# Weight low parts on VectorE alone, constant products that read ones, and a new order of work

## The chip, the core and the metric

The kernel runs on one core of a Trainium2 chip. A core has TensorE (PE in the profile; its weight loads are listed as PEld), VectorE (DVE), ScalarE (ACT), GpSimd (POOL) and SyncE (SP), which issues the transfers. Each engine works through its own instructions in program order and waits by semaphores for the others. The metric is the device time of one execution in microseconds, as a median over several runs.

## The reference

Two stages, one behind the other. The first is clustered attention on `q`, `k`, `v` of shape 4 x 8 x 768 x 64 (batch, heads, tokens, head size) with 16 centroids a head:

```
q_assign = argmax(normalised q . normalised centroids)      # the same for k
mask     = q_assign[:, None] == k_assign[None, :]
scores   = where(mask, (q @ k.T) / sqrt(64), -1e9)
attn     = exp(scores - max);  attn = attn / (sum(attn) + 1e-9)
out      = attn @ v
```

The second takes the 3072 tokens of 512 values that come of it, as `x`, through two large products with a rational function between them:

```
h = x @ w_in                                                # 3072 x 2048
g = (a0 + a1 h + a2 h^2 + a3 h^3) / (1 + |b0||h| + |b1| h^2 + 1e-6)
out = g @ w_out                                             # 3072 x 512
```

`w_in` (512 x 2048) and `w_out` (2048 x 512) come as 64-bit floats. They and all large operands are split into a high and a low part of 16 bits, and a product is the sum of three: high by high, high by low, low by high.

## The kernel before

**The order is written out by hand.** Nothing runs while the kernel is described: each step is a call of `op`, which appends it to a plan (`Plan`, 4453 steps). `emit` then walks through `ORDER`, a list of 4453 numbers, and issues the steps in that sequence. The rows of an engine's instructions stand in the order in which its steps come in that list. A step may issue several instructions.

**The weights** (`weights`, called eight times: four column groups of `w_in`, named `wi0` to `wi3`, four row groups of `w_out`, `wo0` to `wo3`; four tiles of 128 x 512 in each, 32 in all). A tile is loaded as 64-bit words into `rwi...` or `rwo...` (512 KB; L423; two buffers), and is made a 32-bit float in `wwi...` or `wwo...`: ScalarE takes the magnitude of the upper words (`m...`), VectorE shifts it and joins it with bits of the lower words (L558, L565), ScalarE takes the sign (`g...`), GpSimd multiplies the two (L574). TensorE then forms the squares of a group's four tiles, and of their sum `root_pow2` makes a scale, a power of two (`wis`, `wos`; its last steps are L496 and L499 on VectorE). With the scale ScalarE writes the high part, `win[:, 0]` or `wout[:, 0]`, and the **low part**, scaled value minus high part, is formed in one of two ways:

- tiles 1 and 3 of a group: one VectorE instruction, L626, that scales and subtracts;
- tiles 0 and 2: two GpSimd instructions, L635, which scales in place, and L642, which subtracts.

Which it is, `share("wdl", c)` decides: with `K['wdl']` at 0.5 it is true for tiles 1 and 3. So of the 32 low parts 16 are VectorE's and 16 GpSimd's. All are written while the first batch's attention runs, and the second stage needs them.

**The first batch** (`prep`, `attend_keys`). Each of its four head pairs is scaled: ScalarE sums squares of `k` and `q` over a row (`sumk`, `sumq`), TensorE turns the sum into a row (`kt`, L1013), VectorE takes its largest value (`km`, L1015), TensorE spreads that to all partitions (`kb`, L1017), and VectorE makes scales of it (`ksc`, `qsc`, L1027 to L1070). The scaled `tk` and `tq` are transposed (for the first pair on TensorE, L980, with `ident16`). Then come the scores, their largest values, a second run of scores, and the values `px` (L1323 in the later batches, L1501 and L1507 in the first). Of `px` the results are made through `rw`: VectorE L1529 and L1536, TensorE, then VectorE L1553, one set for each head pair and each third of the tokens (`rw_1_0`: pair 1, first third). They end as `x` (GpSimd, L1561). The later batches (`attend`) use scores `s` (L1243), their smallest value (VectorE L1272), the exponential (ScalarE) and `ah`, the split result (ScalarE, then VectorE L1303), which frees the scores' bank.

**The second stage** (`moe`) runs for thirds of a batch: `ph` = x @ w_in (L1612), the rational function (ScalarE, VectorE L1630, L1637, L1731, GpSimd L1677, L1750), `po` = g @ w_out (L1761). It reads columns `gk` of numbers that `g_scale` makes from the scales of the weights, of `v` and from `moe_a`, `moe_b`, in small GpSimd steps (L850, L899, L902). The second stage of one batch runs among the attention of the next.

**The constant products** (`warm`, 16 calls). Each call is a group of eight TensorE products 128 x 128 whose result nobody reads (L786). They read `ident16`, an identity in 16 bits, which VectorE casts from `ident` (L390). TensorE's first instructions are eleven such groups.

Of the kernel before, what the change touches and what calls it, by code (L numbers as in the profile page):

```python
# [57 lines left out]
K = {'xn': 14, 'scp': 1, 'vsc': 0.75, 'sup0': 0, 'stk': 2, 'lop': 0, 'mgp': 0, 'rvn': 2, 'at': 3, 'vn': 3, 'ah': 5, 'sua': 1.0, 'T1': 1, 'quick': 1, 'sqd': 0.0, 'gld': 0.0, 'gp': 0.3, 'pp': 0.0, 'NR': 19, 'acb': 1.0, 'warm': 16, 'fast': 16, 'pet': (0,), 'wdl': 0.5}  # L58
# [200 lines left out]
def clustered_attention_moe_kernel(  # L259
# [75 lines left out]

    def kshare(name, b, i):
        return share(name if f"{name}.{b}" not in K else f"{name}.{b}", i)

    TOGETHER = kn('together', ())

    KEYMAJOR = {(b, hp) for b in range(B) for hp in range(kn("km", (4, 0, 0, 0))[b])}

    plan.look = kn("look", 40.0)
    NM = 2
    NR = kn("NR", 12 if kn("gw", 1) == 1 else 6)

    def misc(shape, dt, name):
# [1506 lines left out]
```

## Time and profile before

| | |
|---|---|
| median of 3 runs | 903.31 us (903.31 to 904.04) |
| the profiled execution, its own time | 900.24 us |
| span of its instructions | 898.4 us |
| busy: TensorE, VectorE, ScalarE, GpSimd | 862.0, 811.3, 794.5, 533.2 us |
| granted TensorE clock over the span | 0.99 |

The profile is of one execution, which took 900.24 us; the span leaves out 1.8 us around its first and last instruction. "Busy" counts an engine's instructions, not its waits, and says nothing of how well an engine is used: TensorE's matmuls overlap and their ends are modelled. A table by stretches of the span gives the same busy time for parts of it. A table of waits gives the idle time of an engine ahead of an instruction and what ended it. A timeline lists instructions in order of their start.

### The profile page before, as it was taken

To read this page: it belongs to the slowest core of one execution; us is meant where nothing else is said; L and a number is where in the kernel's file an instruction comes from. 1 tells how busy PE (TensorE), PEld (TensorE's weight loads), DVE (VectorE), ACT (ScalarE), POOL (GpSimd) and SP (SyncE) were. 2 spreads that over 40 slices of the span, in tenths; PEclk is the share of its full clock that TensorE was granted. 3 is DMA by queue.
4 is the path that set the end of the run, shared out by engine and by line. 5 is a ranking of instruction groups with operands and counts; after the bars stand their busy time and mean duration, and the time that the engine had idled before them with its cause. 6 is when DMAs were issued, how large, how long until landed. Compare 5 with 4: busy or idle time off the path is not lost.

```text
span 898.4 us, 20920 instructions
## 1 busy us (share of the span) xinstructions
PE 862.0 (96%) x7893; PEld 594.4 (66%) x7893; DVE 811.3 (90%) x1610; ACT 794.5 (88%) x1497; POOL 533.2 (59%) x530
## 2 busy tenths in 40 slices
PE   5699999988999999999999999999999999999998
PEld 4566777765666666657667666667676666767654
DVE  3999989789999999989999999999999998877793
ACT  4688899999999999999999999999999999895652
POOL 2337645677766385547556737565666555687664
PEclk9799999999999999999999999999999999999999
DMA  4698876779877999886979999989789875150000
GB/s 155 190 251 216 198 186 144 206 146 210 160 139 139 191 198 183 190 161 127 216 153 167 178 189 171 159 169 179 152 154 170 156 139 95 36 95 1 24 24 24
DMA packets 353013, 135.76 MB, mean 151 GB/s; under 512 B 327824, under 2 KB 344208, under 8 KB 352912
## 3 DMA queue, kind: packets, MB, share of 16 engines
q1 hardware_dynamic: 352912, 134.42, 74.0%
q8 instruction: 62, 1.02, 0.4%
q14 instruction: 39, 0.32, 0.1%
HBM read 41.98 MB, written 6.29 MB: 54 GB/s over the span
## 4 chain that ended last, share of the span: by engine, by line
PE 61%; DVE 17%; ACT 14%; issue 5%; POOL 1%; DMA 1%; SPq 1%; ACTq 0%; DVEq 0%
PE po L1761 20%; PE ph L1612 19%; PE s L1243 7%; PE px L1323 5%; DVE s L1272 3%; ACT s L409 3%; DVE ah L1303 3%; ACT u L409 2%; ACT ah L409 2%; PE s L1386 2%; PE z L1480 2%; PE px L1501 2%; DVE t L1637 1%; DVE t L1630 1%; PE ptl L1138 1%
## 5 line engine op out<-in xcount | busy, mean ns | idle before, releaser
L1612 PE MATMUL ph<-x,win 128*128 128x256 f16 x2304 | 266.2, 273 | 1.1 <-DVE t L1637 0.6
L1761 PE MATMUL po<-wout,g 128*128 128x512 f16 x1152 | 267.1, 379 | 0.0
L1612 PEld LDWEIGHTS <-win 128*128 128x128 f16 x2304 | 223.9, 98 | 42.0 <-DVE t L1637 2.9
L1761 PEld LDWEIGHTS <-g 128*128 128x128 f16 x1152 | 110.5, 98 | 120.1 <-issue 3.4
L1750 POOL TENSOR_TENSOR g<-t,u 128x512 f16<-128x512 f32 x84 | 112.7, 1344 | 93.8 <-DVE t L1743 56.6
L1677 POOL TENSOR_TENSOR s<-s,u 128x512 f32<-128x512 f32 x84 | 111.2, 1329 | 74.9 <-ACT s L409 73.1
L1272 DVE TENSOR_SCALAR_CACHE_REDUCE s<-s,cc 128x768 f32<-128x768 f32 x144 | 144.9, 1018 | 4.4 <-PE s L1243 3.5
L1303 DVE SCALAR_TENSOR_TENSOR ah<-s,su,ah 128x768 f16<-128x768 f32 x144 | 144.1, 1010 | 4.4 <-ACT ah L409 3.9
L409 ACT ACTIVATE ah<-s,su 128x768 f16<-128x768 f32 x144 | 127.8, 899 | 6.6 <-DVE su L1291 6.1
L409 ACT ACTIVATE s<-s,nm 128x768 f32<-128x768 f32 x144 | 125.6, 872 | 8.4 <-DVE s L1272 6.5
L1243 PE MATMUL s<-sk,sq 128*128 128x384 f16 x576 | 115.6, 327 | 6.3 <-DVE ah L1303 5.6
L1243 PEld LDWEIGHTS <-sq 128*128 128x128 f16 x576 | 52.0, 98 | 49.9 <-DVE ah L1303 16.4
L1323 PE MATMUL px<-at,vhi 128*64 128x256 f16 x864 | 73.9, 275 | 1.9 <-DVE s L1731 1.8
L409 ACT ACTIVATE t<-ph,gk 128x512 f32<-128x512 f32 x84 | 65.3, 778 | 0.0
L1630 DVE SCALAR_TENSOR_TENSOR t<-ph,gk,t 128x512 f32<-128x512 f32 x84 | 62.2, 742 | 2.5 <-ACT t L409 1.4
L1637 DVE SCALAR_TENSOR_TENSOR t<-t,gk,ph 128x512 f32<-128x512 f32 x84 | 62.3, 741 | 1.2
L409 ACT ACTIVATE u<-s,cq 128x512 f32<-128x512 f32 x84 | 59.8, 721 | 3.0 <-POOL s L1677 2.9
L409 ACT ACTIVATE s<-u,g 128x512 f32<-128x512 f32 x84 | 60.3, 723 | 0.5
L409 ACT ACTIVATE u<-ph,gk 128x512 f32<-128x512 f32 x84 | 57.7, 688 | 3.3 <-PE ph L1612 3.1
L1731 DVE SCALAR_TENSOR_TENSOR s<-s,g 128x512 f32<-128x512 f32 x84 | 59.8, 714 | 0.5
L1323 PE MATMUL px<-at,vlo 128*64 128x256 f16 x432 | 59.7, 273 | 0.0
L1323 PEld LDWEIGHTS <-vhi 128*64 128x64 f16 x864 | 45.0, 110 | 15.3 <-issue 10.3
(241 smaller groups left out, 1552.4 us busy)
## 6 DMA issues: line engine op xcount, KB each, us to landing
rwi<-in_moe_w_in_dram SPq DMA_DIRECT2D x16, 512.0 KB, 3.9
rwo<-in_moe_w_out_dram SPq DMA_DIRECT2D x16, 512.0 KB, 4.3
rk<-in_k_dram SPq DMA_DIRECT2D x32, 192.0 KB, 3.9
rq<-in_q_dram SPq DMA_DIRECT2D x32, 192.0 KB, 3.7
rvm<-in_v_dram SPq DMA_DIRECT2D x16, 384.0 KB, 4.0
rv<-in_v_dram SPq DMA_DIRECT2D x16, 384.0 KB, 4.1
out_dram<-ob SPq DMA_DIRECT2D x24, 256.0 KB, 2.9
sq<-sq SPq DMA_DIRECT2D x12, 192.0 KB, 4.1
```

The lines of the kernel that those rows point to most:

```text
L409: lambda: nc.scalar.activation(out=out(), in_=in_(), func=func, **{a: (x() if callable(x) else x) for a, x in kw.items()}),
L1243: nc.tensor.matmul(sc.ap[:, i, :SH], lhsT=st["q" + x].ap[:, j, t, :], rhs=st["k" + x].ap[:, j, ks, :].rearrange("p t c -> p (t c)"), start ...
L1272: lambda nm=nm, view=view: ts(out=view(), in0=view(), scalar1=cc.ap[:, 0:1], scalar2=None, op0=ALU.mult, op1=ALU.min, accum_out=nm.ap),
L1303: lambda part=part, view=view, su=su: stt(out=part(1), in0=view(), scalar=su.ap, in1=part(0), op0=ALU.mult, op1=ALU.subtract),
L1323: nc.tensor.matmul(px.ap[j * D : (j + 1) * D, :], lhsT=vv.ap[:, j, kt, :], rhs=at[j].ap[:, p_, kt].rearrange("p t c -> p (t c)"), start=(i ...
L1612: nc.tensor.matmul(ph.ap[:, fi * TW : (fi + 1) * TW], lhsT=win[:, wpart, c, f * P : (f + 1) * P], rhs=xs[c].ap[:, xpart], start=(i == 0), ...
L1630: lambda t=t, h=h, ph=ph, col=col: stt(out=t[h].ap, in0=ph.ap, scalar=col("rho")(), in1=t[h].ap, op0=ALU.mult, op1=ALU.mult),
L1637: lambda t=t, h=h, ph=ph, col=col: stt(out=t[h].ap, in0=t[h].ap, scalar=col("a1")(), in1=ph.ap, op0=ALU.add, op1=ALU.mult),
L1677: lambda uv=uv, sv=sv: nc.gpsimd.tensor_tensor(out=sv(), in0=sv(), in1=uv(), op=ALU.mult),
L1731: lambda sv=sv, g16=g16: stt(out=sv(), in0=sv(), scalar=1.0 + 1e-6, in1=g16(0), op0=ALU.add, op1=ALU.mult),
L1750: lambda tv=tv, uv=uv, g16=g16, e=(nc.vector if kshare("gld", b, i_) else nc.gpsimd): e.tensor_tensor(out=g16(1), in0=tv(), in1=uv(), op=A ...
L1761: nc.tensor.matmul(po[ti].ap, lhsT=g16(gg)[:, c0 : c0 + P], rhs=wout[:, wpart, f, :], start=(i == 0 and f == 0), stop=(i == 2 and f == NF ...
```

## The change

- `K['wdl']` goes from 0.5 to 1.0: L626 (L628 in the new numbering, which is two higher from there) forms all 32 low parts. L635 and L642 are no longer issued: 32 fewer GpSimd instructions, 16 more of VectorE, and 4437 steps for 4453.
- The constant products read `w16w`, a tile of ones in bfloat16 that a VectorE memset fills, for `ident16`. `ident16` is now made on GpSimd (a memset and a select, by `make_identity`), not cast on VectorE.
- `ORDER` is another list from end to end.
- The set `KEYMAJOR` is written in another way and holds the same four head pairs.

```diff
-K = {..., 'warm': 16, 'fast': 16, 'pet': (0,), 'wdl': 0.5}
+K = {..., 'warm': 16, 'fast': 16, 'pet': (0,), 'wdl': 1.0}
...
 ORDER = [int(i) for i in """
+4438 4450 40 41 42 43 4437 4447 4445 4449 4444 4443 4452 4448 44 3 4 74 75 5 6 76 77 78 79 386 387 389 4451
...
-    KEYMAJOR = {(b, hp) for b in range(B) for hp in range(kn("km", (4, 0, 0, 0))[b])}
+    KEYMAJOR = {(0, hp) for hp in kn("kmset", (0, 1, 2, 3))}
...
     ident16 = cp.tile([P, P], F16, name="ident16")
-    nc.vector.tensor_copy(out=ident16, in_=ident)
+    make_identity(nc, ident16)
+    w16w = cp.tile([P, P], BF16, name="w16w")
+    nc.vector.memset(w16w, 1.0)
...
             for _ in range(8):
-                nc.tensor.matmul(wm.ap[:, :P], lhsT=ident16, rhs=ident16, start=True, stop=True)
+                nc.tensor.matmul(wm.ap[:, :P], lhsT=w16w, rhs=w16w, start=True, stop=True)
```

What the new order and the new instructions make of the rows is shown at three places. In a row the name stands ahead of its inputs (`out<-in`); a number at a name's end is that of a buffer and differs between the two kernels for that reason alone.

**The head of VectorE's instructions**, from the second weight tile to the first scale `ksc`. Before:

```order
L444 TENSOR_TENSOR csq<-craw 128x64
L445 TENSOR_REDUCE css<-csq 128x1
L448 TENSOR_SCALAR cn<-css 128x1
L558 TENSOR_SCALAR wwo_1_222<-mwo_1_218 128x512
L565 SCALAR_TENSOR_TENSOR wwo_1_222<-rwo_1_216,wwo_1_222 128x512
L390 CAST ident_85<-ident 128x128
L1015 TENSOR_REDUCE km_0_245<-kt_0_243 1x1
L1027 TENSOR_SCALAR ksc_0_249<-kb_0_247 128x1
```

After (in the new numbering; `w16w` is filled five rows above the first of these):

```order
L560 TENSOR_SCALAR wwi_2_122<-mwi_2_120 128x512
L567 SCALAR_TENSOR_TENSOR wwi_2_122<-rwi_2_118,wwi_2_122 128x512
L560 TENSOR_SCALAR wwo_1_186<-mwo_1_184 128x512
L567 SCALAR_TENSOR_TENSOR wwo_1_186<-rwo_1_182,wwo_1_186 128x512
L446 TENSOR_TENSOR csq<-craw 128x64
L1017 TENSOR_REDUCE km_0_249<-kt_0_247 1x1
L447 TENSOR_REDUCE css<-csq 128x1
L450 TENSOR_SCALAR cn<-css 128x1
L1029 TENSOR_SCALAR ksc_0_264<-kb_0_262 128x1
```

The cast of `ident16` (`ident_85`) is gone from here; `km` stands behind the same two weight tiles as before, and of the centroids' three steps two now come behind it.

**VectorE around the results of the second head pair** (`rw_1_0`, `rw_1_1`), the same row numbers in both. Before:

```order
L1553 SCALAR_TENSOR_TENSOR rw_1_0_1712<-px_1_0_1675,ev_1171,rw_1_0_1712 128x256
L1027 TENSOR_SCALAR qsc_0_1830<-sumq_0_1828 128x1
L1529 SCALAR_TENSOR_TENSOR rw_1_1_1869<-px_1_1_1832,eps,rw_1_1_1869 128x128
L1536 SCALAR_TENSOR_TENSOR rw_1_1_1869<-rw_1_1_1869 128x128
L1015 TENSOR_REDUCE km_0_1890<-kt_0_1888 1x1
L1027 TENSOR_SCALAR ksc_0_1911<-kb_0_1909 128x1
L558 TENSOR_SCALAR wwo_3_1917<-mwo_3_1915 128x512
L565 SCALAR_TENSOR_TENSOR wwo_3_1917<-rwo_3_1913,wwo_3_1917 128x512
L626 SCALAR_TENSOR_TENSOR wout<-wwo_1_1196,wos,wout 128x512
L1040 TENSOR_SCALAR ksc_0_1911<-ksc_0_1911 128x1
L1045 RECIPROCAL ksc_0_1911<-ksc_0_1911 128x1
L1050 TENSOR_SCALAR qsc_0_1830<-ksc_0_1911 128x1
```

After:

```order
L1538 SCALAR_TENSOR_TENSOR rw_1_0_1681<-rw_1_0_1681 128x128
L628 SCALAR_TENSOR_TENSOR win<-wwi_2_1037,wis,win 128x512
L498 TENSOR_SCALAR woe<-wop_ln 128x1
L501 RECIPROCAL wos<-woe 128x1
L1531 SCALAR_TENSOR_TENSOR rw_1_1_1849<-px_1_1_1812,eps,rw_1_1_1849 128x128
L1538 SCALAR_TENSOR_TENSOR rw_1_1_1849<-rw_1_1_1849 128x128
L628 SCALAR_TENSOR_TENSOR wout<-wwo_2_572,wos,wout 128x512
L560 TENSOR_SCALAR wwo_3_1857<-mwo_3_1810 128x512
L1555 SCALAR_TENSOR_TENSOR rw_1_0_1681<-px_1_0_1644,ev_1204,rw_1_0_1681 128x256
L628 SCALAR_TENSOR_TENSOR win<-wwi_3_498,wis,win 128x512
L567 SCALAR_TENSOR_TENSOR wwo_3_1857<-rwo_3_1808,wwo_3_1857 128x512
L560 TENSOR_SCALAR wwo_0_1900<-mwo_0_1898 128x512
```

Where one low part (L626) stood in twelve rows, three stand now (L628), two of `w_in` and one of `w_out`, between the steps of `rw_1_0` and `rw_1_1`.

**GpSimd's steps of `gk`**, the last ones ahead of the first `ph`. Before:

```order
L850 TENSOR_SCALAR gk_2428<-woe,g_2430 128x4
L850 TENSOR_SCALAR g_2430<-g_2430 128x1
L635 TENSOR_SCALAR wwi_2_1487<-wwi_2_1487,wis 128x512
L850 TENSOR_SCALAR g_2430<-g_2430,aab 128x1
L850 TENSOR_SCALAR gk_2428<-gk_2428,g_2430 128x4
L899 TENSOR_TENSOR gk_2428<-gk_2428 128x4
L1561 TENSOR_TENSOR x_2_1_2464<-rw_2_1_2360,x_2_1_2464 128x256
L850 TENSOR_SCALAR gk_2428<-gk_2428,ab 128x4
L642 TENSOR_TENSOR wout<-wwo_2_2049,wout 128x512
L642 TENSOR_TENSOR win<-wwi_2_1487,win 128x512
L850 TENSOR_SCALAR gk_2428<-gk_2428,ab 128x4 x2
L635 TENSOR_SCALAR wwo_2_1344<-wwo_2_1344,wos 128x512
```

After:

```order
L852 TENSOR_SCALAR g_2424<-g_2424 128x1
L852 TENSOR_SCALAR g_2424<-g_2424,aab 128x1
L852 TENSOR_SCALAR gk_2422<-gk_2422,g_2424 128x4
L1563 TENSOR_TENSOR x_1_2_2799<-rw_1_2_1965,x_1_2_2799 128x256
L901 TENSOR_TENSOR gk_2422<-gk_2422 128x4
L852 TENSOR_SCALAR gk_2422<-gk_2422,ab 128x4 x4
L904 TENSOR_TENSOR gk_2422<-gk_2422 128x4
L1563 TENSOR_TENSOR x_3_0_2970<-rw_3_0_2719,x_3_0_2970 128x256
```

The four instructions of low parts (L635, L642) that stood between the `gk` steps are gone, and the result `x_1_2` (L1563) stands there now.

## Rows read from the trace of the kernel before

**Rows 1.** The page, part 1: busy us, share of the span, instructions.

```profile
PE 862.0 (96%) x7893; PEld 594.4 (66%) x7893; DVE 811.3 (90%) x1610; ACT 794.5 (88%) x1497; POOL 533.2 (59%) x530
```

**Rows 2.** Stretches: length, each engine's busy us, then TensorE's clock, DMA share, GB/s.

```profile
0.00:20.00 20.00, 8.80 (x111) 8.12 (x112) 6.08 (x30) 8.39 (x16) 5.05 (x18) 0.99 0.44 140
20.00:60.00 40.00, 32.15 (x324) 23.97 (x326) 37.45 (x99) 29.08 (x52) 12.91 (x13) 0.79 0.82 229
60.00:100.00 40.00, 39.39 (x456) 27.25 (x453) 39.42 (x84) 34.35 (x62) 26.66 (x26) 1.00 0.87 205
100.00:200.00 100.00, 96.30 (x1253) 72.14 (x1252) 86.19 (x196) 94.35 (x183) 59.58 (x74) 1.00 0.75 176
200.00:400.00 200.00, 192.06 (x1648) 129.54 (x1647) 193.59 (x380) 194.23 (x381) 125.52 (x120) 1.00 0.92 177
400.00:880.00 480.00, 479.30 (x4043) 326.90 (x4042) 444.23 (x820) 429.50 (x802) 295.81 (x274) 1.00 0.69 129
```

**Rows 3.** TensorE's waits, 200 to 400 us: sum, times, longest.

```profile
PE s L1243 <- DVE ah L1303: 4.9, 5, 1.9
```

**Rows 4.** Timeline, first 20.5 us: start, length, engine [idle before, releaser].

```profile
0.83 0.17 DVE L374 MEMSET ones<- 128x128 f32 x1 [0.83 <-PEq L1838]
...
8.32 0.69 DVE L565 SCALAR_TENSOR_TENSOR wwo<-rwo,wwo 128x512 int32<-128x512 int32 x1
...
8.93 0.22 DVE L390 CAST ident<-ident 128x128 f16<-128x128 f32 x1
...
9.02 0.19 ACT L409 ACTIVATION_READ_ACCUMULATOR tk<-rk 128x1 f32 x1
...
9.08 0.34 SPq L423 DMA_DIRECT2D rwi<-in_moe_w_in_dram  x1
...
9.21 1.03 PE L786 MATMUL warm-39.99_113<-ident 128*128 128x128 f16 x8 [9.21 <-DVE ident L390]
...
12.60 0.63 PE L786 MATMUL warm-39.92_156<-ident 128*128 128x128 f16 x8
...
15.75 0.27 PE L1013 MATMUL kt<-ident,sumk 128*1 128x128 f32 x1
...
16.05 0.28 DVE L1015 TENSOR_REDUCE km<-kt 1x1 f32<-1x128 f32 x1 [6.90 <-PE kt L1013]
...
19.88 0.66 ACT L409 ACTIVATE mwi<-rwi 128x512 f32<-128x512 f32 x1
```

**Rows 5.** Loads into `rwi`, first 60 us: from issue to landing.

```profile
DMA to landing us min/median/max: 3.6/3.9/5.6
```

**Rows 6.** Lines L626 and L565: ns min/median/max, first and last start.

```profile
L626 DVE SCALAR_TENSOR_TENSOR win<-wwi,wis,win x8: 731/742/1173, 84.1 to 182.4; 128x512 f16<-128x512 f32 x8
L626 DVE SCALAR_TENSOR_TENSOR wout<-wwo,wos,wout x8: 721/744/917, 104.3 to 192.6; 128x512 f16<-128x512 f32 x8
...
L565 DVE SCALAR_TENSOR_TENSOR wwo<-rwo,wwo x16: 674/691/1639, 8.3 to 167.2; 128x512 int32<-128x512 int32 x16
```

**Rows 7.** GpSimd's groups by line and form: busy us, mean ns, idle before.

```profile
L642 POOL TENSOR_TENSOR win<-wwi,win 128x512 f16<-128x512 f32 x8 | 10.9, 1356 | 0.3
...
L642 POOL TENSOR_TENSOR wout<-wwo,wout 128x512 f16<-128x512 f32 x8 | 9.5, 1196 | 0.3
...
L635 POOL TENSOR_SCALAR wwo<-wwo,wos 128x512 f32<-128x512 f32 x8 | 5.8, 722 | 4.1 <-DVE rest L1437 3.2 <-ACT wout L409 0.9
...
L635 POOL TENSOR_SCALAR wwi<-wwi,wis 128x512 f32<-128x512 f32 x8 | 5.7, 711 | 0.1
```

**Rows 8.** Timeline, 181 to 192 us, of GpSimd and of TensorE.

```profile
182.55 0.68 POOL L850 TENSOR_SCALAR gk<-woe,g 128x4 f32<-128x4 f32 x1 [5.66 <-DVE g L894]
...
190.38 1.36 PE L1612 MATMUL ph<-x,win 128*128 128x256 f16 x11
```

**Rows 9.** VectorE's waits, 60 to 200 us.

```profile
DVE rw L1529 <- ACT rw L409: 2.2, 3, 1.1
```

**Rows 10.** A stretch of 5 us, columns as in rows 2.

```profile
30.00:35.00 5.00, 3.38 (x33) 3.41 (x34) 4.89 (x12) 5.00 (x9) 2.49 (x3) 0.50 0.29 89
```

More of the change, by code (lines that the diff above doesn't have):

```diff
@@ L55, in emit @@
             self.ops[i]()
-K = {'xn': 14, 'scp': 1, 'vsc': 0.75, 'sup0': 0, 'stk': 2, 'lop': 0, 'mgp': 0, 'rvn': 2, 'at': 3, 'vn': 3, 'ah': 5, 'sua': 1.0, 'T1': 1, 'quick': 1, 'sqd': 0.0, 'gld': 0.0, 'gp': 0.3, 'pp': 0.0, 'NR': 19, 'acb': 1.0, 'warm': 16, 'fast': 16, 'pet': (0,), 'wdl': 0.5}
+K = {'xn': 14, 'scp': 1, 'vsc': 0.75, 'sup0': 0, 'stk': 2, 'lop': 0, 'mgp': 0, 'rvn': 2, 'at': 3, 'vn': 3, 'ah': 5, 'sua': 1.0, 'T1': 1, 'quick': 1, 'sqd': 0.0, 'gld': 0.0, 'gp': 0.3, 'pp': 0.0, 'NR': 19, 'acb': 1.0, 'warm': 16, 'fast': 16, 'pet': (0,), 'wdl': 1.0}
 ORDER = [int(i) for i in """
[193 rows of a table removed]
[193 rows of a table added]
 """.split()]
```

386 rows, old and new, of the table ORDER are left out of this document.

## The prediction

> **What bounds the kernel now.** Read the busy table first, then the same by stretches of the span, then the waits. TensorE is busy 862.0 us of 898.4, VectorE 811.3 [rows 1]. The stretches tell what that average hides [rows 2]. From 400 to 880 us TensorE is idle 0.7 us of 480: whatever is won or lost before 400 us arrives at the end one for one, and nothing can be won behind it but the last few us. From 200 to 400 us TensorE lacks 7.9 us and VectorE only 6.4; the score products wait there for VectorE's `ah` instruction, which frees their bank (4.9 us in 5 waits [rows 3]). So this stretch goes at VectorE's pace. From 20 to 100 us VectorE is all but full too (2.6 us idle of 40, then 0.6 of 40). From 100 to 200 us it has 13.8 us idle, while TensorE (96.3) and ScalarE (94.4) are nearly full. And at the front, TensorE does 8.8 us of work in the first 20.
>
> The front is one chain. TensorE starts at 9.21 us, because its first constant product reads `ident16`, which VectorE casts at 8.93, behind weight arithmetic that waits for a load [rows 4]. Eleven groups of eight constant products then stand ahead of the first useful transpose, `kt`, and they run to 15.75. ScalarE had the sum that `kt` reads at 9.21 (9.02 + 0.19). VectorE stands still for 6.90 us until 16.05, its next instruction being the one that reads `kt`, and ScalarE waits behind that (all [rows 4]).
>
> **The change, part by part.**
>
> *Constant products read ones.* The new `w16w` is a VectorE memset ahead of everything that waits for a load; the memset of `ones`, same elements, takes 0.17 us and stands at 0.83 [rows 4]. TensorE can start near 1.4. The first four of the eleven groups start 0.85 us apart (9.21 to 12.60 is 3.39), the other seven 0.45 (12.60 to 15.75 is 3.15) [rows 4]: 6.5 us, done at 7.9 instead of 15.75. Last then is ScalarE's sum at 9.21, and `kt` can run at 9.25: 6.5 us earlier. If all eleven ran at the pace of the first four, they would end at 1.4 + 9.35 = 10.75 and the gain be 5.0. I take 6.5, since the pace should rise after as long a run as it did before. One group is moved between `kt` and `kb`; `kb` needs VectorE's `km` first (16.05 + 0.28 [rows 4]), so 0.45 us of it is hidden, 0.85 nearly. The identity moves to GpSimd, as a memset and a select ahead of its first weight tile; nobody waits for it before the transposes of `tk`, which in this trace come after 16.05. What is late next: the load of the third weight tile is issued at 9.08 [rows 4] and lands after a median 3.9 us, at most 5.6 [rows 5]: 13.0 to 14.7. ScalarE reads it at 19.88 [rows 4], so at 13.4 if all moves by 6.5. Median: in time; worst: 1.3 us late. So the front gives 6.5, between 3.7 and 6.5. VectorE being full from 20 to 100 us, work that starts earlier there ends earlier.
>
> *All low parts on VectorE.* Sixteen more instructions of the form of L626, median 742 and 744 ns [rows 6]. Back to back, VectorE's instructions start about 0.08 us before the one ahead has ended (8.32 + 0.69 is 9.01, the next starts at 8.93 [rows 4]), so one costs 0.66 and sixteen 10.6 us; without that overlap 11.9. GpSimd loses 16 pairs, 10.9 + 9.5 + 5.8 + 5.7 = 31.9 us [rows 7], which is worth little in itself: GpSimd is busy 59% [rows 1].
>
> *Where they stand.* By the new order 30 of the 32 low parts are ahead of the first hidden product `ph`, where all 16 of VectorE's were: 14 more, 9.3 us, nearly all of it between the second head pair's results and `ph` at 190 [rows 8]. That is the stretch with 13.8 us of idle VectorE. All of it could be covered, or none. I take 8 of 10.6 us: the stretches where VectorE sets the pace keep 1.4% (60 to 100) to 3.2% (200 to 400) idle [rows 2]; with ScalarE and TensorE nearly full I allow this one some 5%, and 13.8 less 5.8 is 8. So 2.6 us stay on the path. If the cover were gone the whole 10.6 would be, since VectorE sets the pace from 200 to 400.
>
> *Less beside GpSimd.* A VectorE instruction is now and then far longer than its like: L565 has a median of 691 ns and a maximum of 1639, L626 742 and 1173 [rows 6], so one such case costs 0.4 to 0.9 us. If they come from GpSimd's work beside them, they get fewer: from 60 to 200 us GpSimd is busy 86.2 us [rows 2], of which 31.9 go, 37%. I take one case of the longer kind, 1.0 us (0 to three of them, 2.8).
>
> *The chain to `ph`.* GpSimd's small `gk` instructions begin at 182.55 and `ph`, which reads `gk`, at 190.38 [rows 8]; four of the removed instructions stand between them: two of each kind, by the group means 2 x (0.71 + 1.28) = 4.0 us [rows 7]. So `ph` could come up to 4.0 us earlier; but TensorE has other products to do ahead of it and few gaps [rows 2], so I count 0 and keep 4.0 for the low end.
>
> **The sum.** 900.24 us (the profiled execution; span 898.4) - 6.5 + 10.6 - 8.0 - 1.0 = 895.3. The median of the runs, 903.31, lies 3.1 above the profiled one, so 898.4 us.
>
> **Rivals.**
>
> *A. VectorE pays in full; slower.* The 13.8 us idle are waits, in program order, for short steps that go through other engines (the longest in sum is `rw` for ScalarE, 2.2 us in 3 waits [rows 9]). More instructions in that queue delay such a step by as much as they fill, and the gap comes back behind it. For it: the waits are many and short; against it: the new order was laid out with the new instructions in it. 900.24 - 6.5 + 10.6 = 904.3, by the median 907.4. It decides when less than 4.1 us of the 10.6 are covered.
>
> *B. The front's gain stops at the next wait.* If the loads or the work of the second head pair hold the front, 2 us of the 6.5 arrive: 895.3 + 4.5 = 899.8, by the median 902.9, within 0.2%.
>
> *C. More than counted.* All 10.6 covered and half of the 4.0 us and a little more off the chain to `ph`, 2.6: 895.3 - 5.2 = 890.1, by the median 893.2.
>
> *D. The clock.* The granted clock is 0.99 in the first 20 us [rows 2] and 0.50, the lower of its two levels (1.2 of 2.4 GHz), from 30 to 35 [rows 10], after stretches in which TensorE had pauses. Constant products that end at 7.9 leave a pause before `kt` and thin work behind it. TensorE's 32.15 us at 0.79 (20 to 60 us [rows 2]) are 25.4 at full rate; at half rate all the way they need 50.8, 10.8 more than the 40 us they have: 909.2. Against it: VectorE, not TensorE, is full there, and the rate was half for part of it already. The Trainium skill (TensorE: Matmul & The Clock Gate, What's actually happening) says that the throttled state is the default and activity releases it; by that an early run that ends early gains nothing for what comes after. This trace agrees that the rate falls again when the run is over [rows 10].
>
> *E. Held by GpSimd.* The new instruction reads two tiles from SBUF, as L626 does now. Were each held as the worst of L626 (1173 ns, 0.43 over the median [rows 6]): 16 x 0.43 = 6.9, so 905.3. The medians, near the fastest (721 and 731 ns [rows 6]), speak against it. The Trainium skill (SBUF — State Buffer, Who interferes with whom) states that such an instruction and a GpSimd one that reads SBUF exclude each other, and the second waits for the whole of the first. The trace agrees in so far as single cases are long, and in no more: by the medians most were held by nothing.
>
> **How the numbers follow.** My forecast 898.4 has a chance of 0.46, with a range of its own from 895 to 901.4; C 0.16; B 0.14; A 0.16; D 0.04; E 0.04. 0.2% is about what a measurement of this kernel can tell from no change, 901.5 to 905.1. Faster: forecast and C, 0.62. Same: B, 0.14. Slower: A, D, E, 0.24. The range reaches into C and just over A, 892 to 907.5: some 0.06 lie below and 0.12 above.
>
> **What would show it.** First constant product near 1.4 us, `kt` near 9.3, VectorE's wait for it under 1 us. VectorE's idle time from 95 to 190 us at 5 to 6 instead of 13.8; L628 at 32 with a median near 743 ns. The first `ph` some 4 to 6 us earlier than 190.4, and TensorE without gaps from 400 on. I am wrong at the front if `kt` comes early but the first scores don't; at the cover if VectorE's idle time stays above 10 us and `ph` comes near 190; in the rest of the order if `ph` is early and the end is not.

## The result

The changed kernel takes 888.85 us (median; 887.65 to 889.21), the kernel before 903.54 beside it: a ratio of 0.9834 with a 95% interval from 0.9817 to 0.9851, or 15 us. Measured once more in a later series (e13) it is 0.9861 (0.9837 to 0.9885), 12.6 us. The forecast was faster by 4.9 us, at 898.4, with a range down to 892.0: the direction was right, but the time lies below the range, and the forecast gain is a third of what came. The profiled execution took 888.94 us with a span of 886.8; before it was 900.24 and 898.4.

The page of the changed kernel, part 1 (busy us, share of the span, instructions), answers to [rows 1], and the table by stretches to [rows 2] (length, busy us of TensorE, its weight loads, VectorE, ScalarE and GpSimd, then clock, DMA share, GB/s).

```profile
PE 860.9 (97%) x7893; PEld 596.3 (67%) x7893; DVE 818.5 (92%) x1626; ACT 795.1 (90%) x1497; POOL 498.4 (56%) x500
```

```profile
0.00:20.00 20.00, 14.79 (x189) 13.70 (x190) 12.77 (x50) 14.48 (x26) 5.83 (x20) 0.91 0.76 240
20.00:60.00 40.00, 34.82 (x349) 24.83 (x346) 38.06 (x95) 31.05 (x56) 16.00 (x15) 0.87 0.84 215
60.00:100.00 40.00, 39.98 (x508) 28.67 (x509) 39.29 (x88) 33.47 (x61) 15.05 (x16) 1.00 0.82 210
100.00:200.00 100.00, 95.71 (x1199) 72.91 (x1197) 94.50 (x209) 96.07 (x188) 45.08 (x61) 1.00 0.68 174
200.00:400.00 200.00, 193.92 (x1709) 132.57 (x1704) 196.08 (x390) 196.47 (x387) 121.46 (x118) 1.00 0.91 173
400.00:880.00 480.00, 479.32 (x3954) 322.75 (x3952) 437.84 (x799) 422.31 (x784) 295.02 (x272) 1.00 0.68 128
```

From 100 to 200 us VectorE is idle 5.5 us where it was 13.8, and TensorE is as busy as it was. From 400 on nothing is left to win, as before.

The front, from the timeline of its first 20.5 us (start, length, engine, in brackets the idle time before and what ended it), answers to [rows 4]:

```profile
1.18 0.17 DVE L392 MEMSET w16w<- 128x128 bf16 x1
...
1.40 1.03 PE L788 MATMUL warm-39.87_124<-w16w 128*128 128x128 bf16 x8 [1.40 <-DVE mrow L394]
...
9.09 0.27 PE L1015 MATMUL kt<-ident,sumk 128*1 128x128 f32 x1
...
9.40 0.28 DVE L1017 TENSOR_REDUCE km<-kt 1x1 f32<-1x128 f32 x1 [0.60 <-PE kt L1015]
...
14.03 0.66 ACT L411 ACTIVATE mwi<-rwi 128x512 f32<-128x512 f32 x1 [0.22 <-DMA rwi<-in_moe_w_in_dram]
```

Constant products from 1.40 us, `kt` at 9.09 (15.75 before), VectorE's wait for it 0.60 (6.90 before), the third weight tile read at 14.03 after a wait of 0.22 for its load.

The new line of the low parts answers to [rows 6] (ns of one: shortest, median, longest; first and last start), and the first hidden products show how early `ph` is:

```profile
L628 DVE SCALAR_TENSOR_TENSOR win<-wwi,wis,win x16: 733/744/1805, 70.0 to 180.3; 128x512 f16<-128x512 f32 x16
L628 DVE SCALAR_TENSOR_TENSOR wout<-wwo,wos,wout x16: 731/746/1770, 98.0 to 189.4; 128x512 f16<-128x512 f32 x16
...
L1614 PE MATMUL ph<-x,win x120: 269/272/283, 180.5 to 198.6; 128*128 128x256 f16 x120
```

The first `ph` stands at 180.5 us, 9.9 earlier than at 190.38 [rows 8]; from there to the end it is 706.3 us now and was 708.0. So most of the gain is made ahead of `ph`.

### The profile page after: what moved, and what is told of

The parts are those of the page before. It is cut to its first block, busy times and chain, and to the rows that moved or that the text cites. A ratio compares the mean times of both kernels' runs of the same rounds, so it can differ in the third digit from the quotient of the medians.

```text
span 886.8 us, 20919 instructions
## 1 busy us (share of the span) xinstructions
PE 860.9 (97%) x7893; PEld 596.3 (67%) x7893; DVE 818.5 (92%) x1626; ACT 795.1 (90%) x1497; POOL 498.4 (56%) x500
## 4 chain that ended last, share of the span: by engine, by line
PE 64%; DVE 16%; ACT 13%; issue 4%; DMA 1%; POOL 0%; ACTq 0%; DVEq 0%; SPq 0%; POOLq 0%
PE po L1763 21%; PE ph L1614 19%; PE s L1245 7%; PE px L1325 6%; ACT s L411 4%; DVE s L1274 3%; DVE ah L1305 2%; ACT ah L411 2%; PE px L1503 2%; ACT u L411 2%; PE s L1388 2%; PE z L1482 2%; DVE top L1398 1%; PE px L1509 1%; DVE s L1733 1%
## 5 line engine op out<-in xcount | busy, mean ns | idle before, releaser
L1325 PEld LDWEIGHTS <-vhi 128*64 128x64 f16 x864 | 44.7, 110 | 13.9 <-issue 9.2
```

Source lines behind the costliest of these rows:

```text
L1325: nc.tensor.matmul(px.ap[j * D : (j + 1) * D, :], lhsT=vv.ap[:, j, kt, :], rhs=at[j].ap[:, p_, kt].rearrange("p t c -> p (t c)"), start=(i ...
```

## The experiments

The theories that the expectations name: **1**, the front gives 6.5 us and the order covers the 16 instructions; **2**, the relief of GpSimd is a gain of its own; **3**, the early start shortens the time at the lower clock; **4**, the order behind `ph` gains too; **5**, the 16 still cost something in the new order; **6** and **7**, the clock or VectorE's lateness is what misplaced instructions cost.

Four marks are read from every trace: the start of `kt`, of the first values `px`, of the first `ph`, and the span.

| | kt | first px | first ph | span | median | ratio to before (95%) |
|---|---|---|---|---|---|---|
| before | 15.75 | 57.9 | 190.4 | 898.4 | 903.5 | 1 |
| changed | 9.09 | 48.7 | 180.5 | 886.8 | 888.9 | 0.9834 (0.9817 to 0.9851) |
| e1 old order, ones, GpSimd pairs | 9.38 | 52.6 | 184.8 | 892.9 | 895.4 | 0.9921 (0.9902 to 0.9941) |
| e2 old order, identity, VectorE's low parts | 16.25 | 58.4 | 196.1 | 909.3 | 913.1 | 1.0120 (1.0097 to 1.0144) |
| e3 old order, ones, VectorE's | 9.27 | 52.5 | 191.3 | 906.5 | 906.3 | 1.0048 (1.0030 to 1.0066) |
| e4 new order, identity, VectorE's | 16.83 | 56.5 | 187.9 | 894.2 | 896.8 | 0.9942 (0.9924 to 0.9961) |
| e5 new order, ones, GpSimd pairs | 8.22 | 48.1 | 189.7 | 895.7 | 897.8 | 0.9941 (0.9929 to 0.9954) |
| e6 new order to ph, then old | 8.02 | 48.3 | 180.5 | 892.0 | 894.0 | 0.9903 (0.9888 to 0.9919) |
| e7 old order to ph, then new | 9.53 | 51.1 | 190.0 | 904.3 | 906.1 | 1.0028 (1.0012 to 1.0043) |
| e8 changed, the 16 twice | 8.48 | 48.2 | 190.9 | 897.4 | 899.2 | 0.9958 (0.9943 to 0.9972) |
| e9 old order, ones, no low parts of tiles 0, 2 | 9.56 | 52.5 | 183.7 | 891.7 | 893.0 | 0.9896 (0.9880 to 0.9913) |
| e10 new order, ones, none of those | 8.27 | 48.0 | 179.8 | 888.5 | 889.3 | 0.9853 (0.9834 to 0.9871) |
| e11 as e3, the low parts in new places | 9.25 | 52.5 | 194.0 | 905.3 | 907.0 | 1.0050 (1.0034 to 1.0066) |
| e12 changed, the low parts in old places | 8.98 | 48.6 | 184.3 | 896.7 | 898.3 | 0.9950 (0.9931 to 0.9970) |
| e13 changed, again | 8.45 | 48.1 | 179.5 | 886.9 | 890.6 | 0.9861 (0.9837 to 0.9885) |
| e14 as e12, with products in the pauses | 8.73 | 48.5 | 183.7 | 894.6 | 897.2 | 0.9939 (0.9918 to 0.9960) |
| e15 changed, with products in the front's pauses | 8.92 | 48.9 | 179.8 | 886.2 | 890.2 | 0.9856 (0.9832 to 0.9881) |
| e16 changed, 9 groups ahead of kt | 8.58 | 48.1 | 179.7 | 887.2 | 890.3 | 0.9864 (0.9838 to 0.9890) |

The runs were made in four series, each with the kernel before beside it: its median was 901.8 us beside e1 to e4, 903.4 beside e5 to e8, 902.7 beside e9 to e12 and 903.1 beside e13 to e16. So versions of different series are compared by their ratios, and a ratio's interval is some 0.2% wide to either side, 2 us. The marks and spans are those of one profiled execution each.

### The edits one by one

**e1, the ones alone.**

```diff
 (ORDER and K as before)
-    nc.vector.tensor_copy(out=ident16, in_=ident)
+    make_identity(nc, ident16)
+    w16w = cp.tile([P, P], BF16, name="w16w")
+    nc.vector.memset(w16w, 1.0)
...
-    nc.tensor.matmul(wm.ap[:, :P], lhsT=ident16, rhs=ident16, start=True, stop=True)
+    nc.tensor.matmul(wm.ap[:, :P], lhsT=w16w, rhs=w16w, start=True, stop=True)
```

Expected:

> The kernel before, its own order and its own split of the low parts; only the constant products read ones, and the identity is made on GpSimd. Theory 1 (the front is worth 6.5 us and no more; what the change gave beyond it came from the new order): 903.5 - 6.5 = 897.0, with the useful work of TensorE 6 to 6.5 us ahead of before from 25 us on and no more later. Rival, theory 3 (the earlier front also brings the full clock back earlier, which gave the 2 us between 30 and 47 us): 903.5 - 8.5 = 895.0, and the granted clock of 40 to 60 us is 1.00 where before has 0.91. If a load holds the front: 901.

Measured 6.4 us less by the medians of this series (901.8 to 895.4). `kt` comes 6.4 earlier, the first `px` 5.3, `ph` 5.6, the end 5.5. Theory 1 holds: what the front gives arrives at the end but for about 1 us, which is lost ahead of `px`. Theory 3's sign is missing: the granted clock from 40 to 60 us is 0.95 and not 1.00, and over the first 60 us it is 0.86 as before.

**e2 and e3, the low parts on VectorE in the old order,** without and with the ones.

```diff
-K = {..., 'wdl': 0.5}
+K = {..., 'wdl': 1.0}
 ORDER (old), for each of the 16 low parts of tiles 0 and 2:
-    the two GpSimd steps (L635, L642)
+    the one VectorE step, in the place of the second
```

> The kernel before, its own order; only the 16 low parts of tiles 0 and 2 are formed by VectorE, each in the place where the second of its two GpSimd instructions stood. Theory 1 (VectorE pays for what its idle time of 100 to 200 us doesn't cover; only a new order covers it well): 2.6 to 10.6 us more, 906 to 914, VectorE's idle time from 95 to 190 us falling from 12.5 to 6 or less. Rival, theory 2 (the 32 instructions that GpSimd loses gain more than VectorE's 16 cost, in any order): no slower than before, 903.5 or less.

> Both edits of the first two runs together in the old order: the change without its new order. By theory 1 their sum, 900 to 907, so that the new order is worth 11 to 18 us against the changed kernel's 888.9. By theory 2 it is 897 or less and the order is worth 8 or less.

e2 is 11.3 us slower than before, e3 10.9 slower than e1: the 10.6 us of the instructions, paid in full. Theory 2 falls for the old order. Only half of it is paid ahead of `ph`: in e2 `ph` comes 5.7 us later than before and the end 10.9.

**e4, the new order without the ones.**

```diff
 (the changed kernel)
-    make_identity(nc, ident16)
-    w16w = cp.tile([P, P], BF16, name="w16w")
-    nc.vector.memset(w16w, 1.0)
+    nc.vector.tensor_copy(out=ident16, in_=ident)
...
-    nc.tensor.matmul(wm.ap[:, :P], lhsT=w16w, rhs=w16w, start=True, stop=True)
+    nc.tensor.matmul(wm.ap[:, :P], lhsT=ident16, rhs=ident16, start=True, stop=True)
```

> The changed kernel with its new order and its low parts, but the constant products read the identity that VectorE casts, as before. Theory 1 (the front is worth 6.5): 888.9 + 6.5 = 895.4. Theory 3 (the early start also shortens the stretch at the lower clock): 888.9 + 8.5 = 897.4. The difference to the kernel before is then what the new order and the low parts gave together, 6 to 8 us.

The two expected times were worked out from a time of another series. By the ratios e4 is 7 to 10 us behind the changed kernel (0.9942 against 0.9861 and 0.9834), by the spans 7.4, which does not tell 6.5 from 8.5. The granted clock over the first 60 us is 0.89 in both traces, so nothing speaks for theory 3. `kt` comes at 16.83 here, 7.7 later than in the changed kernel. The products start at 9.19, as before, but six of the eleven groups start 0.85 us apart here and only four did before. Yet the first `px` is at 56.5, earlier than before (57.9), though `kt` is 1.1 later. The new order makes up 2.5 us between the two marks.

### What the low parts cost in each order

**e5, GpSimd's pairs in the new order; e8, the 16 twice.**

```diff
 (e5: the changed kernel)
-K = {..., 'wdl': 1.0}
+K = {..., 'wdl': 0.5}
 ORDER (new): the two GpSimd steps where VectorE's one stood
...
 (e8: the changed kernel, L628)
-    lambda hl=hl, wf=wf: stt(...),
+    lambda hl=hl, wf=wf, c=c: [stt(...) for _ in range(2 - c % 2)],
```

> The changed kernel with its new order and its products of ones, but the low parts of tiles 0 and 2 are two GpSimd instructions again, both standing where VectorE's one stood. Theory 1 (the new order covers VectorE's 16 instructions and gains by itself; which engine forms the low parts then matters little): 887 to 890, at most 2 us from the changed kernel. Rival, theory 2 (GpSimd's 31.9 us in these places hold somebody up, so that giving them to VectorE is a gain of its own): 893 to 898. Rival, theory 5 (VectorE's 16 instructions still cost part of their 10.6 us in the new order): 880 to 886.

> The changed kernel with each of the 16 moved low parts formed twice over, one instruction behind the other: 10.6 us more of VectorE in the places where the new order put them. If the new order had cover to spare, 889 to 892; if it is filled by the 16 it has (VectorE's idle time from 85 to 180 us is 5.4 us now), 894 to 900, that is 5 to 10.6 us more.

e5 misses theory 1 and lies in theory 2's range: in the new order GpSimd's pairs do hold somebody up. They cost 8.9 us by the span against VectorE's 16 (8.0 by the ratios against e10 below, which has neither), all of it between `px` (48.1) and `ph` (189.7). Among ScalarE's waits from 95 to 200 us of e5 (what waits, for whom: us in sum, times, longest) are 6 us for GpSimd's second instruction. `gwo`, `rw` and the weight tile that this one reads take their buffers from one ring of 19, and ScalarE waits until one is free:

```profile
ACT gwo L404 <- POOL wout L637: 3.9, 2, 2.0
ACT rw L404 <- POOL win L637: 2.1, 1, 2.1
```

In the changed kernel's waits of that stretch no line of a low part stands. In e8 the 16 instructions a second time cost 9 to 11 us (0.9958 against 0.9861 and 0.9834), their full price, also all ahead of `ph` (190.9). The new order has no room for 16 more.

**e9 and e10, without the low parts of tiles 0 and 2.**

```diff
 (e9: old order; e10: new order; both with the ones)
+    if c % 2 == 0:
+        op("POOL", 500, lambda hl=hl: nc.gpsimd.memset(hl.ap[:, 1], 0.0), [], [hl], vt)
+        continue
```

> Old order, products of ones, and no low parts of tiles 0 and 2 at all (left out of the computation: a GpSimd memset that waits for nothing fills each with zeros). Beside the first run (with the GpSimd pairs, 895.4) and the third (with VectorE's instructions, 906.3) it prices both ways in the old order. If the pairs cost nothing there: 895. If they held something up too: 888 to 893. Either way VectorE's 16 cost the rest up to 906.3, at least 11 us.

> The same in the new order, beside the changed kernel (888.9) and the fifth run (pairs, 897.8). If VectorE's 16 instructions are covered in the new order: 888 to 889. If they cost there what they cost in the old order, as the eighth run (16 more, +10.3) suggests: 877 to 880, and the order alone, with nothing to cover, is worth 10 us or more against the ninth run.

Here is the answer. In the **old order** the work of none, of GpSimd's pairs and of VectorE's 16 gives 0.9896, 0.9921 and 1.0048: 2.3 us for the pairs (the intervals of e9 and e1 overlap), 13.7 for VectorE's. In the **new order** none gives 0.9853 and VectorE's 16 give 0.9834 and 0.9861: nothing, within some 2 us. So the same 16 instructions cost 13.7 us in one order and next to none in the other. And the order alone, with nothing to cover, is worth 0.9896 to 0.9853, 3.9 us; these two intervals don't overlap.

How the one order covers them and the other not stands in VectorE's busy time from 95 to 175 us (third figure after the length), of e9, e3, e10 and the changed kernel:

```profile
95.00:175.00 80.00, 79.55 (x1053) 59.89 (x1053) 69.20 (x158) 75.85 (x142) 39.14 (x46) 1.00 0.75 184
```

```profile
95.00:175.00 80.00, 77.88 (x1033) 58.13 (x1031) 70.01 (x158) 73.98 (x136) 40.26 (x44) 1.00 0.76 188
```

```profile
95.00:175.00 80.00, 79.13 (x1087) 59.65 (x1084) 66.67 (x157) 75.25 (x143) 42.21 (x65) 1.00 0.76 194
```

```profile
95.00:175.00 80.00, 78.66 (x1083) 59.41 (x1080) 75.26 (x170) 74.54 (x142) 37.69 (x51) 1.00 0.74 193
```

In the old order VectorE stands still 10.8 us without the 16 and 10.0 with them; in the new order it is 13.3 us without and 4.7 with them, at the same work of TensorE. To read this, one has to know how many of the 16 stand in that stretch at all. Counted by their starts in the traces (VectorE's low parts, 16 without the moved ones and 32 with them):

| | ahead of 95 us | 95 us to first ph | behind ph | VectorE idle, 95 us to ph | TensorE idle, 95 us to ph |
|---|---|---|---|---|---|
| e9 old order, none of the 16 | 1 | 14 | 1 | 11.8 | 2.1 |
| e3 old order, the 16 | 7 | 19 | 6 | 12.8 | 4.9 |
| e11 old order, 13 of them moved (below) | 4 | 25 | 3 | 12.3 | 9.0 |
| e10 new order, none of the 16 | 1 | 13 | 2 | 13.9 | 2.1 |
| changed: new order, the 16 | 2 | 27 | 3 | 5.3 | 2.8 |
| e12 new order, the 16 in old places (below) | 4 | 21 | 7 | 14.0 | 4.5 |

Of the 16 the new order has 14 in the stretch in which VectorE has idle time, and e3 has only 5 there: 6 stand ahead of it and 5 behind the first `ph`. In both of those places VectorE has nothing to spare; in e9 it is idle 0.5 us of 35 from 60 to 95 us and 0.3 of 25 from 190 to 215:

```profile
60.00:95.00 35.00, 34.13 (x382) 24.01 (x380) 34.51 (x73) 30.12 (x56) 15.06 (x19) 1.00 0.79 214
190.00:215.00 25.00, 21.47 (x177) 14.98 (x177) 24.66 (x49) 24.97 (x48) 16.15 (x18) 1.00 1.00 184
```

So a good part of what e3 pays has nothing to do with that idle time. By the spans 7.1 us of its 14.8 against e9 come behind `ph`, where TensorE waits 4.8 us in one piece for VectorE's `ah`; and from 60 to 95 us TensorE already stands still 2.3 us more. That idle time inside the stretch does not by itself cover an instruction is shown by e11 and e12, which have 11 and 8 of the 16 there: VectorE is idle as long as without them, and TensorE stands still for longer. In the new order 14 instructions take 8.6 us of idle time out of the stretch. The waits of VectorE from 95 to 190 us say which. First e10, then the changed kernel, the longest of each:

```profile
DVE top L1393 <- PE s L1383: 3.0, 3, 1.8
DVE rw L1526 <- ACT rw L403: 2.4, 2, 1.3
DVE tq L1086 <- ACT tq L403: 1.3, 1, 1.3
DVE su L1288 <- ACT su L403: 1.2, 2, 0.7
```

```profile
DVE rw L1531 <- ACT rw L411: 1.1, 2, 0.9
DVE km L1017 <- PE kt L1015: 0.8, 1, 0.8
DVE top L1398 <- PE s L1388: 0.7, 3, 0.3
```

The instructions stand where these waits were. The rows shown of the change had an example: L628 behind L1538 of `rw_1_0`, while that goes through TensorE and ScalarE, and ahead of L1555, which waits for it.

**e11 and e12, the places exchanged.**

```diff
 (e11: e3; e12: the changed kernel)
 ORDER: only the 16 VectorE steps of tiles 0 and 2 moved
-    where this order has them
+    where the other order has them, by the TensorE work ahead of them
```

> Old order, products of ones, VectorE's low parts; but 13 of the 16 (all but the first tile of wi0, of wo0 and of wo1, for which a buffer is missing then) stand where the new order has them, counted by the TensorE work ahead of them. If the place of these instructions is what the new order's gain is made of: 890 to 896 (third run: 906.3). If the gain comes from how the other instructions were laid: 902 to 907.

> The counterpart: the new order, but the 16 low parts as far as their high parts allow where the old order's GpSimd pairs stood, by TensorE work (most of them earlier than in the new order, 6 between 60 and 110 us). If the place decides: 898 to 904. If the order of the others does: 889 to 892.

e12 is 8 to 10 us slower than the changed kernel (0.9950 against 0.9861 and 0.9834), so the place decides in the new order. Here `ph` comes 4 to 5 us later, and the rest is lost behind it, where another `ph` waits 4.8 us in one piece for VectorE. But e11 gains nothing on e3: the same places, counted roughly by TensorE's work, are no gaps in the old order. Whether a finer choice would cover them there was not tried.

**e6 and e7, half of each order.** The steps ahead of the first `ph` are the same in both orders but for 9 and 5.

```diff
 ORDER (e6)
-    the 4437 steps of the new order
+    the first 1015 of the new order, then the rest as the old order has them
 ORDER (e7)
+    the steps up to the first ph as the old order has them, then the rest of the new
```

> All edits of the change; the new order up to the first hidden product ph (1015 of 4437 steps, some 190 us), the old order of the remaining steps behind it. Theory 1 (the order's gain is made ahead of ph): 889 to 891. Rival, theory 4 (the 4 us that the changed kernel gains between 200 and 400 us come from the order of the steps there): 892 to 894.

> The complement: all edits, the old order up to the first ph, the new order behind it. The old order with all edits took 906.3. Theory 1: 904 to 906.5, since the VectorE instructions stay uncovered ahead of ph. Theory 4: 901 to 903.

e6 keeps `ph` at 180.5 and then loses 5 us; its 894.0 is the time of theory 4. e7 is 1.8 us ahead of e3 by the ratios, within their intervals; its 906.1 is the time of theory 1. So the two don't agree on what the order behind `ph` is worth, and a seam may cost by itself. That share isn't shown.

### Is it TensorE's clock?

In e8 and e12 TensorE's pauses around the first `ph` are followed by stretches at 0.50, the lower level (186.4 to 193.2 us in e8, 181.1 to 187.9 in e12). e14 fills the pauses of e12 with constant products, e15 some of those in the changed kernel's front.

```diff
 (e14: e12; e15: the changed kernel)
+    def warm_o(i):        # as warm, in another bank
...
 ORDER
+    e14: 2 groups ahead of vt, 3 ahead of vb, 8 and 2 ahead of the two ph that waited
+    e15: 14 groups ahead of the transposes, sums and scores that TensorE waited for, 10 to 31 us
```

> The twelfth run (new order, low parts in the old places, 898.3) with 15 more groups of constant products in the pauses that TensorE made there from 178 to 212 us: 2 ahead of vt, 3 ahead of vb, 8 and 2 ahead of the two hidden products that waited. They add no wait, since TensorE stood still. Theory 6 (a good part of the 10 us that misplaced instructions cost is the clock, at half rate from 181 to 188 and from 204 to 209 us after such pauses): 893.5 to 896. Rival, theory 7 (VectorE's lateness sets the pace there and the clock is hidden behind it): 898 to 899.

> The changed kernel with 14 more groups of constant products in the pauses that TensorE makes from 10 to 31 us, where its clock is at half rate for 13 us in sum. If the rate there sets the end (theory 6 at the front): 884 to 887. If VectorE does, full there as it is: 888.5 to 890, with the granted clock of 10 to 36 us near 1.

From 180 to 188 us, e12 and then e14 (the clock is the third figure from the end):

```profile
180.00:188.00 8.00, 6.60 (x73) 5.45 (x74) 6.82 (x17) 5.58 (x15) 1.51 (x2) 0.57 0.31 67
```

```profile
180.00:188.00 8.00, 7.27 (x106) 5.95 (x104) 7.40 (x17) 6.18 (x17) 1.62 (x2) 1.00 0.39 76
```

The clock rises from 0.57 to 1.00, and by the ratios the time falls by 1 us of the 8 to 10 (0.9950 to 0.9939; 2.1 by the spans), inside the uncertainty. 897.2 lies between the two theories' times, nearer to theory 7's. At the front the clock goes from 0.56 (e13) to 0.99 (e15) between 10 and 20 us, and the median moves by 0.4; from 20 to 30 us it stays low, 0.59 and 0.67, so e15 is a test of half of that stretch:

```profile
10.00:20.00 10.00, 7.08 (x92) 6.00 (x92) 8.58 (x30) 9.71 (x18) 0.86 (x4) 0.56 0.83 262
```

```profile
10.00:20.00 10.00, 8.01 (x142) 6.85 (x141) 8.55 (x31) 9.30 (x17) 0.53 (x3) 0.99 0.78 246
```

Theory 6 falls: where the clock was raised, 1 to 2 of the 8 to 10 us came back around `ph`, and nothing that can be told from zero at the front. That leaves theory 7, VectorE's lateness; no run tests it by itself.

**e13 and e16.** e16 leaves out two of the eleven groups ahead of `kt`.

```diff
 (e16: the changed kernel)
-K = {..., 'warm': 16, ...}
+K = {..., 'warm': 14, ...}
```

> The changed kernel once more, so that the next three are compared with it on one chip. All theories: 0.983 to 0.985 of before.

> The changed kernel with 9 groups of constant products ahead of kt and not 11. They ended at 9.09 us and the sum that kt reads was there at 8.2. If the first step waits for them: kt at 8.2, the end 0.5 to 0.9 us earlier. If VectorE's two weight tiles ahead of km (done at 8.6) hold it, or the thinner run of products costs clock: no gain, 888.5 to 890.

890.6 and 890.3. e13's ratio of 0.9861 is a little above the 0.983 to 0.985 expected, within its interval. `kt` moves between 8.0 and 9.1 us in the runs with ones in the new order, and nothing follows from it: the first `px` stands at 48.0 to 48.9 in all of them. No version beats the changed kernel by more than the uncertainty.

### What the order alone gains

e9 and e10 part before the low parts begin: both start their first score product at 29.1 us, and the first `px` is at 52.5 and 48.0. From there to `ph` they take 131.2 and 131.8 us, from `ph` to the end 708.1 and 708.7: the order's gain is made between the first score and the first `px`. The trace before had the sign of it. From its first score product to its first `px` (35.84 to 57.90), and from the changed kernel's (29.81 to 48.70):

```profile
35.84:57.90 22.06, 18.86 (x179) 12.46 (x177) 21.10 (x53) 13.72 (x27) 8.30 (x9) 0.91 0.99 253
```

```profile
29.81:48.70 18.89, 17.88 (x170) 12.23 (x169) 18.18 (x44) 13.08 (x26) 5.20 (x7) 0.91 0.86 228
```

VectorE is full in both, with 53 instructions in one and 44 in the other. And TensorE's waits in the first of them held the first line below, which the second lacks. The next two are the same wait in e9 and in e10, from 29 to 53 us:

```profile
PE s L1386 <- DVE top L1396: 2.3, 3, 1.3
PE s L1383 <- DVE top L1393: 3.5, 3, 1.7
PE s L1383 <- DVE top L1393: 1.2, 2, 0.7
```

The scores waited for VectorE's `top`, which frees their bank, and `px` stood behind more of VectorE's work than it needed. In the new order it comes 3 us sooner after the first score than before, and 4.4 sooner in e10 than in e9. This is read from the traces; no run moved these instructions alone.

## Why the prediction was wrong

**The front (6.5 us, between 3.7 and 6.5): right.** e1 gave 5.5 by the span, 6.4 by the medians and 7.1 by the ratio. All three checks named for it came true: 1.40 us, 9.09, 0.60. In e1 the products end near 7.9 and `kt` waits for ScalarE's sum, as the working has it. In the profiled execution of the changed kernel it was the other way round, and that `kt` still came near 9.25 is luck: more groups ran at the slow pace, and the products ended at 9.09, not 7.9, while the sum was there at 8.19, not 9.21.

**The price of the 16 instructions (10.6 us): right.** e2 11.3, e3 10.9, and the same again for the second 16 in e8. Their median, forecast at 743 ns, is 744 and 746.

**The cover (8.0 of it): what it left on the path is the first step that failed.** The forecast filled 8.0 us of VectorE's idle time and let the other 2.6 of the 10.6 us lengthen the kernel. The idle time was foreseen right: 8.3 us less of it from 100 to 200 us than before, and 5.5 left (5.5 from 95 to 190 too, where it had been 12.5 and not 13.8). But the 2.6 us are not found in the time: against e10 the 16 instructions cost from -1.7 to +0.7, within some 2 us. So the term was too small by about its 2.6 us, which is as much as these ratios can just tell. I had worked it out as a share of idle time to be filled; what the runs show is that each instruction's place counts. Rival A's mechanism is real: e11 and e12 show it, with 11 and 8 more instructions in the stretch and as much idle time as without them. The old order pays A's price and more (e3), in part because 11 of the 16 stand there where VectorE has no idle time. What I held against A, that the new order was laid with the instructions in it, is what decided; it should have carried the whole 10.6.

**Less beside GpSimd (1.0, between 0 and 2.8): the size fits, the reason isn't shown.** e9 is 2.3 us faster than e1 by the ratios, whose intervals overlap, and 1.2 by the spans. That GpSimd's work beside them makes VectorE's instructions long is seen in the traces. In each of the two, before and changed, 7 instructions of L565 and L626 (now L567 and L628) took over 0.75 us. Each of these began while a GpSimd instruction ran and ended 0.54 to 0.56 us after that one had ended. The longest L628:

```profile
143.48 1.27 POOL L576 TENSOR_TENSOR wwo<-wwo,gwo 128x512 f32<-128x512 f32 x1 [2.58 <-ACT gwo L411]
143.50 1.80 DVE L628 SCALAR_TENSOR_TENSOR win<-wwi,wis,win 128x512 f16<-128x512 f32 x1
```

The Trainium skill (SBUF — State Buffer, Who interferes with whom) has the second of two such instructions wait for the whole of the first, and these rows agree. But the cases on these lines, to which 16 instructions were added, did not get fewer, and what they take above the medians rose from 3.0 to 4.4 us: other GpSimd instructions, here the sign's multiplication, met L628 as well. What the pairs did hold is shown in the new order only: ScalarE, by a buffer that they still read (e5).

**The chain to `ph` (0, up to 4.0): right.** `ph` is 9.9 us earlier, and the marks account for it ahead of the chain: the first `px` is 9.2 earlier already. In the old order taking GpSimd's pairs away brings `ph` 1.1 us forward (e1 to e9).

**The new order itself: put at nothing, the second step that failed and the larger one.** It is worth 3.9 us with nothing to cover (e9, e10), and it is made between the first scores and the first `px`. The prediction counted the order as a list of places for 16 instructions; what it does with all the others has no term there, and no reason is given. A wait of 2.3 us in TensorE's row, in the very stretch where I had called VectorE full, was not followed up.

**The median over the profiled execution (+3.1): not a property of the kernel.** This was the third miss, of 3.1 us in the sum. The execution that was profiled before lay low in the spread of that kernel (899.9 to 906.0 in all later runs); that of the changed kernel, 888.94, lies on its median. From one profiled execution to the other the change is 11.3 us, from median to median 14.7 here and 12.6 in e13.

So -6.5 - 1.0 + 2.6 = -4.9 was forecast. The runs, each compared with the one before it, give by ratios -7.1 (e1), -2.3 (e9), -3.9 (e10) and from -1.7 to +0.7 for the 16 in the new order, -15 to -12.6 together; by the spans -5.5, -1.2, -3.2 and -1.7, -11.6 together. These add up to the whole by the way they are formed; what they show is how it divides. By the ratios all four came out better than forecast, the order by more than its uncertainty. The miss of 9.5 us from 898.4 to 888.9 is about the order's 3.9, the offset's 3.1 and the cover's 2.6. C, which had all 10.6 us covered, was the nearest rival at 893.2. It came nearer in part by luck: its other 2.6 us were to come off the chain to `ph`, and it lacked the order.

**What stays open.** The share of the order behind `ph`: e6 loses 5 us without it, e7 gains 1.8 with it, and both have a seam. Why the places of the new order, as e11 took them over, are no gaps in the old one. And why the 16 cost 13.7 us in e3, more than their own 10.6: the loss wasn't followed from instruction to instruction.

## What to carry to other kernels

Idle time of an engine that works in program order covers an added instruction only if the instruction stands where that idle time is. Count first how many of the new instructions the order puts into the stretch that has it: the same 16 cost 13.7 us in one order, which has 5 of them there, and next to nothing in another, which was laid with them and has 14 there. The right stretch alone isn't enough: in e11 and e12 11 and 8 of them stood in it at other places, the idle time stayed what it was, and the time was lost again. When a change brings a new order, price the order as a change of its own: mark the first use of each stage, and look in the old trace for the short waits between the marks that other rows could remove. And add no offset from one profiled execution to a median when the spread of single runs is as large as the offset.

## What the hardware showed beside

TensorE's granted clock at 0.50 cost little where VectorE was late anyway. For 7 us around `ph` in e12, raising it to 1.00 with products in the pauses moved the time by 1 us, by the ratios. In the changed kernel's front it is at 0.50 for 13 to 17 us; raising it from 10 to 20 us moved the time by 0.4. Both are inside the uncertainty. The clock isn't the same in each execution of one program either: e13 is the changed kernel, has 0.56 from 10 to 20 us where the changed kernel's other profile has 0.83, and the spans are 886.9 and 886.8.
